# Float16 pairs for the gated layer of an attention, expert and gated-layer kernel

## The chip, the cores and the metric

The kernel runs as one program on one core of a Trainium2 chip. The metric is the device time of one execution in microseconds (us), the median of several runs. "PE" is TensorE, "PEld" its weight load, DVE is VectorE, ACT is ScalarE, POOL is GpSimd and SP is SyncE, which issues all transfers here.

## The reference

Three layers follow each other. Inputs are float32, except the three matrices of the gated layer's weights, which reach the kernel as float64 words and are turned into float32 on the chip.

```python
# attention: q, k, v (2, 8, 576, 64); heads 0-3 see 32 local positions, heads 4-7 every 32nd
attn = softmax(where(mask, q @ k.T / 8, -1e9)); x = (attn @ v) as (1152, 512)
# experts: 4 of 512 -> 1024 -> 512, all tokens through all experts
for e in range(4):
    out += p[:, e:e+1] * (maximum(x @ w1[e], 0) @ w2[e])
# gated layer: 512 -> 1536 -> 512
return (sigmoid(x @ w_gate) * (x @ w_val)) @ w_out
```

## The kernel before

**Split products.** Every float32 operand is a pair: a rounded high part and the rest as a low part. `split_products` makes one product out of three passes (high x high, high x low, low x high; L543 to L545) that add up in PSUM. The pairs are fp32r tiles (32-bit) or float16 tiles. In float16 the operand is first multiplied by a power of two that brings its largest magnitude to a fixed height, and the result is scaled back.

**Stages.** The expert layer is 8 stages `s` (4 experts, two halves of 512 hidden columns), the gated layer 3 stages `j` (512 hidden columns each). Tokens go in 3 blocks `T` of 384. A unit is a stage and a block: `g1` ("u") makes the hidden tile in 4 groups of 12 passes of 384 columns, `g2` ("d") brings it down in 4 such groups and adds it to `x2`. In the gated layer `g3` has 8 such groups (gate and value by turns), and `g4` 3 groups of 12 passes of 512 columns. The units run in the order u(s,1), d(s,0), u(s,2), d(s,1), u(s+1,0), d(s,2) and so on. Stages 0 and 1 (`EARLY` = 2) run on fp32r pairs, stages 2 to 7 on float16 pairs, the gated stages on fp32r pairs again.

**Weights.** There are 25 pieces of 512 x 512 weights. SP loads each as raw tiles of 512 KB, two to a piece in the expert stages, four (float64 words) in the gated ones; `RAW_BUFS` = 3 of these tiles exist. `prep_weights` makes the pairs: by `prep_half` for the float16 stages (two reductions for the largest magnitude, `scale_on_chip`, then per 512 columns an ACT pass and a DVE pass), by `float32_of` (five DVE passes, L323 to L332) and a copy on ACT and a subtraction on POOL (L350) for a gated tile. A prepared piece takes a buffer of each of the two tags `wh` and `wl`, of which there are five (`W_BUFS` + `W_BUFS_2`), and a float16 piece fills half of its two buffers. `prep_half` gives its two raw tiles back when the whole piece is done.

**Scale.** `scale_on_chip` has two small products: PE turns the 128 per-partition maxima into a row (L243), DVE takes the maximum and keeps its exponent, PE spreads it over the partitions (L248), DVE makes the factor and its inverse. Between the steps it says "hold", which ends the preparation for that group.

**Order.** The program is written under a manual schedule: what is emitted first comes first in each engine's queue. After the last pass of a group (`"evac"`) the loop at the end lets `prep_some` emit two steps of weight preparation (and in units 4 to 10 one step of `x_half`, the splitting of `x` for the float16 stages), and only then the group's own work on the result is emitted. A piece starts only when its buffer's last reader has been emitted (`free_after`). So PE meets a small product of a scale one group after DVE was given the reduction that it needs.

Of the kernel before, what the change touches and what calls it, by code (L numbers as in the profile page):

```python
# [22 lines left out]
TOP = 2.0 ** 14  # L23
# [15 lines left out]
def attn_moe_glu_kernel(ctx, tc, q, k, v, dp, w1, w2, wg, wv, wo, out):  # L39
# [109 lines left out]
    one = nc.const_aps.tensor(1.0, (128, 1), F32)  # L149
    SX = 2 * NST  # L150
# [76 lines left out]
    def as_half(s):  # L227

        return EARLY <= s < NST
# [3 lines left out]
    def alloc_scales():  # L233

        for name, n in (("up", SX + NT), ("down", SX + NT), ("comb", NST * NT), ("top", 2)):
# [49 lines left out]

    held_raw = {}

    def prep_half(n):
# [14 lines left out]
        pool = tmp["w"] if pool_of.get(i) == "w2" else wp  # L303
        wh[i] = pool.tile([128, 4, 512], F16, tag="wh", name="wh")
        wl[i] = pool.tile([128, 4, 512], F16, tag="wl", name="wl")
# [7 lines left out]
        for k_ in ((i, 0), (i, 2), i):  # L313
            held_raw.pop(k_)
        load_raw_to(n + 1 + RAW_BUFS)

    def float32_of(r):
# [4 lines left out]
        m = tmp["p"].tile([128, 512], U32, tag="magn", name="magn")  # L322
# [11 lines left out]
        return f.unsqueeze(1)  # L334

    def prep_weights(n):
        i, u, m = raw_list[n]
        if as_half(i // 2):
            yield from prep_half(n)
            return  # L340
        if u == 0:
            pool = tmp["w"] if pool_of.get(i) == "w2" else wp
            wh[i] = pool.tile([128, 4, 512], F32R, tag="wh", name="wh")
            wl[i] = pool.tile([128, 4, 512], F32R, tag="wl", name="wl")
        r = raw.pop((i, u))
        hi_, lo_ = wh[i][:, u:u + m, :], wl[i][:, u:u + m, :]
        if m == 1:
            r = yield from float32_of(r)
            nc.scalar.copy(hi_, r)  # L349
            nc.gpsimd.tensor_tensor(lo_, r, hi_.bitcast(F32), ALU.subtract)  # L350
        else:
            for x in range(m):
                nc.scalar.copy(hi_[:, x], r[:, x])
                yield
                nc.vector.tensor_tensor(lo_[:, x], r[:, x], hi_[:, x].bitcast(F32), ALU.subtract)
                yield
# [191 lines left out]
    def up_pairs(pc, T, fb):  # L548
        xs = (xh16, xl16) if as_half(pc // 2) else (xh, xl)
# [5 lines left out]
    def alloc_h(key):  # L555
        dt = F16 if key[0] != "g" and as_half(key[0]) else F32R
# [23 lines left out]
    def g2(s, T):  # L580
        e, pc = s // 2, 2 * s + 1
        if s == NST - 1:
            alloc_x(T)
# [6 lines left out]
        for kk in range(KC):  # L590
# [19 lines left out]
            if s == NST - 1:  # L610
                dh, dl = xh[T][:, kk, :], xl[T][:, kk, :]
                nc.scalar.copy(dh, a)
                nc.vector.tensor_tensor(dl, a, dh.bitcast(F32), ALU.subtract)
            yield "tile"

    def g3(j, T):
        base = 2 * NST + 3 * j
        alloc_h(("g", j, T))
        for fb in range(4):
# [4 lines left out]
            nc.scalar.activation(sg, pg, AF.Sigmoid)  # L624
# [6 lines left out]
            nc.vector.tensor_tensor(gv, pv_, sg, ALU.mult)  # L631
            nc.scalar.copy(dh, gv)  # L632
            nc.gpsimd.tensor_tensor(dl, gv, dh.bitcast(F32), ALU.subtract)  # L633
            yield "tile"

    def g4(j, T):
        pc, key = 2 * NST + 3 * j + 2, ("g", j, T)
# [196 lines left out]
```

## Time and profile before

| | |
|---|---|
| median of 3 runs | 716.91 us (712.18 to 731.52) |
| profiled execution, first to last instruction | 712.1 us |
| PE busy | 697.7 us |
| DVE, ACT, POOL busy | 453.4, 237.9, 211.2 us |
| granted TensorE clock, mean | 0.978 |

The profiled execution has no time of its own beside its span; the lowest run, 712.18 us, is the nearest to it. Read the table with the chain of work that ended last in mind: it runs through PE's passes up to the last addition, so time is lost where PE idles or runs at a lower clock, and where a pass takes longer than it has to.

### The profile page before, as it was taken

The page shows a single profiled execution, that of the slowest core. Times are in us where ns is not written, and L with a number is a line of the kernel's source. Part 1 is how long each engine was busy: PE and PEld are TensorE (multiplying, and loading weights), DVE is VectorE, ACT ScalarE, POOL GpSimd, SP SyncE. Part 2 cuts the span into 40 slices and gives each one's busy share as a digit, 9 for nine tenths or more (in the row PEclk, how much of TensorE's full clock was granted, in tenths as well). Part 3 has the DMA queues.
Part 4 walks back from the last instruction along what each step waited for, and adds up shares of the span by engine and source line. Part 5 has one row for each costly group of instructions (what it writes and reads, how often), then busy time and mean ns, then how long its engine had stood idle before and what let it go on. Part 6 is the DMA issues. An engine that isn't in the chain of part 4 may idle for free. (4 is left out here: it accounts for less than half of the span.)

```text
span 712.1 us, 10883 instructions
## 1 busy us (share of the span) xinstructions
PE 697.7 (98%) x4263; PEld 545.2 (77%) x4263; DVE 453.4 (64%) x857; ACT 237.9 (33%) x629; POOL 211.2 (30%) x218
## 2 busy tenths in 40 slices
PE   8999999999789999999999999999999999999998
PEld 5778889999466666656656666678999999999996
DVE  3677665888656565574565889978794777571212
ACT  4675551333313331333333222333234332221120
POOL 2452450000212222222222335542254443442120
PEclk8888999999999999999999999999999999999999
DMA  8933123021221102220121212212122123100002
GB/s 189 216 93 88 59 74 100 18 67 39 70 71 60 60 1 70 71 69 3 60 71 44 75 60 90 90 60 73 45 89 90 60 88 92 58 31 0 30 16 89
DMA packets 38940, 48.58 MB, mean 68 GB/s; under 512 B 18436, under 2 KB 23336, under 8 KB 38888
## 3 DMA queue, kind: packets, MB, share of 16 engines
q1 hardware_dynamic: 38888, 47.89, 23.3%
q8 instruction: 33, 0.54, 0.3%
q14 instruction: 19, 0.16, 0.1%
HBM read 45.50 MB, written 2.38 MB: 67 GB/s over the span
## 5 line engine op out<-in xcount | busy, mean ns | idle before, releaser
L566 POOL TENSOR_TENSOR hl<-t,hh 128x384 f16<-128x384 f32 x72 | 70.5, 984 | 248.6 <-ACT t L565 248.6
L543 PE MATMUL gps<-xh,wh 128*128 128x384 f32 x384 | 130.9, 341 | 0.4 <-DVE gv L631 0.4
L545 PE MATMUL gps<-xh,wl 128*128 128x384 f32 x384 | 128.9, 336 | 0.0
L544 PE MATMUL gps<-xl,wh 128*128 128x384 f32 x384 | 128.8, 335 | 0.0
L543 PE MATMUL gps<-hh,wh 128*128 128x384 f16 (+1 forms) x384 | 127.6, 332 | 0.6 <-ACT sg L624 0.6
L544 PE MATMUL gps<-hl,wh 128*128 128x384 f16 (+1 forms) x384 | 126.0, 328 | 0.0
L545 PE MATMUL gps<-hh,wl 128*128 128x384 f16 (+1 forms) x384 | 126.0, 328 | 0.0
L545 PE MATMUL gps<-x,wl 128*128 128x384 f16 x288 | 95.0, 330 | 0.0
L544 PE MATMUL gps<-x,wh 128*128 128x384 f16 x288 | 94.9, 329 | 0.0
L543 PE MATMUL gps<-x,wh 128*128 128x384 f16 x288 | 94.8, 329 | 0.0
L545 PEld LDWEIGHTS <-wl 128*128 128x128 f16 x576 | 56.6, 98 | 37.7 <-issue 0.7
L543 PEld LDWEIGHTS <-wh 128*128 128x128 f16 x576 | 56.5, 98 | 37.4 <-issue 1.0
L544 PEld LDWEIGHTS <-wh 128*128 128x128 f16 x576 | 56.6, 98 | 37.1 <-issue 1.3
L564 ACT ACTIVATE hh<-gps 128x384 f16<-128x384 f32 x72 | 35.3, 490 | 123.9 <-PE gps L545 123.9
L350 POOL TENSOR_TENSOR wl<-magn,wh 128x512 fp32r<-128x512 f32 x36 | 51.5, 1431 | 76.4 <-ACT wh L349 76.3
L543 PEld LDWEIGHTS gps<-xh,wh 128*128 128x128 f32 x384 | 72.4, 189 | 2.1 <-DVE gv L631 0.7
L544 PEld LDWEIGHTS gps<-xl,wh 128*128 128x128 f32 x384 | 72.4, 189 | 0.3
L545 PEld LDWEIGHTS gps<-xh,wl 128*128 128x128 f32 x384 | 72.2, 188 | 0.0
L633 POOL TENSOR_TENSOR hl<-gv,hh 128x384 fp32r<-128x384 f32 x36 | 43.0, 1194 | 96.5 <-ACT hh L632 96.4
L606 DVE SCALAR_TENSOR_TENSOR t<-gps,comb,pb 128x384 f32<-128x384 f32 x72 | 44.1, 613 | 37.6 <-PE gps L545 20.6
L631 DVE TENSOR_TENSOR gv<-gps,sg 128x384 f32<-128x384 f32 x36 | 20.0, 555 | 60.7 <-PE gps L545 55.5
L609 DVE TENSOR_TENSOR x2acc<-x2acc,t 128x384 f32<-128x384 f32 x84 | 50.9, 606 | 2.9
(113 smaller groups left out, 1073.3 us busy)
## 6 DMA issues: line engine op xcount, KB each, us to landing
raw<-in_moe_w_dram SPq DMA_DIRECT2D x32, 512.0 KB
raw<-in_moe_w_gate_dram SPq DMA_DIRECT2D x12, 512.0 KB
raw<-in_moe_w_val_dram SPq DMA_DIRECT2D x12, 512.0 KB
raw<-in_moe_w_out_dram SPq DMA_DIRECT2D x12, 512.0 KB
pb<-pd SPq DMA_DIRECT2D x11, 192.0 KB
out_dram<-outacc SPq DMA_DIRECT2D x8, 256.0 KB
vl<-in_v_dram SPq DMA_DIRECT2D x8, 160.0 KB
vs<-in_v_dram SPq DMA_DIRECT2D x4, 288.0 KB
```

The lines of the kernel that those rows point to most:

```text
L350: nc.gpsimd.tensor_tensor(lo_, r, hi_.bitcast(F32), ALU.subtract)
L543: nc.tensor.matmul(ps, ah, bh, start=i == 0, stop=False)
L544: nc.tensor.matmul(ps, ah, bl, start=False, stop=False)
L545: nc.tensor.matmul(ps, al, bh, start=False, stop=i == n - 1)
L564: nc.scalar.activation(dh, ps, AF.Relu, scale=DOWN)
L566: nc.gpsimd.tensor_tensor(dl, t, dh, ALU.subtract)
L606: nc.vector.scalar_tensor_tensor(t, ps, cc, pb[e, T], ALU.mult, ALU.mult)
L609: nc.vector.tensor_tensor(a, a, t, ALU.add)
L631: nc.vector.tensor_tensor(gv, pv_, sg, ALU.mult)
L633: nc.gpsimd.tensor_tensor(dl, gv, dh.bitcast(F32), ALU.subtract)
```

## The change

The gated layer's products go from fp32r pairs to scaled float16 pairs. For that `x2` is split by `x2_half` (two reductions, a scale, four ACT and four DVE passes per block), queued behind the last expert stage and emitted at two steps per group, with no weight preparation in those groups; before, the copy and the subtraction of `x2` stood in `g2`. A gated piece now holds four converted tiles (`magn`, five buffers), has a reduction per tile and a scale, and is split by two ACT passes and one POOL subtraction per tile. The scale is found with one bfloat16 product that carries the 128 maxima to every partition at once. A float16 piece takes one buffer for both parts, so that ten fit instead of five. A fourth raw tile exists from the end of the attention on, and `prep_half` gives its first raw tile back halfway. The factors are taken out in the sigmoid's scale, in the gated product's multiplication and in `g4`'s addition. While `x_half` runs, weights get one step per group; in the gated stages they get three.

```diff
+    late = []
+
     def load_raw_to(n):
+        n += len(late)
         while raw_next[0] < min(n, len(raw_list)):
             i, u, m = raw_list[raw_next[0]]
-            t = rawp.tile([128, m, 512], F32 if m == 2 else U64, tag="raw", name="raw")
+            pool = rawp
+            if late and (raw_next[0] - late[0]) % (RAW_BUFS + 1) == 0:
+                pool = tmp["p"]
+            t = pool.tile(
+                [128, m, 512], F32 if m == 2 else U64, tag="raw", name="raw", bufs=RAW_BUFS if pool is rawp else 1)
...
-        return EARLY <= s < NST
+        return s >= EARLY
...
     def scale_on_chip(col, m):
 
+        ps = g_tile()
+        top = m.bitcast(BF16)[:, 1:2]
+        nc.tensor.matmul(ps[:, :128], top.to_broadcast([128, 128]), identb, start=True, stop=True)
+        t = tmp["top"][:, n_top[0] % 2:n_top[0] % 2 + 1]
         n_top[0] += 1
-        t = tmp["top"][:1, n_top[0] % 2:n_top[0] % 2 + 1]
-        ps = g_tile()
-        nc.tensor.transpose(ps[:1, :128], m, ident)
-        nc.vector.tensor_reduce(t, ps[:1, :128], AX.X, ALU.max)
+        nc.vector.tensor_reduce(t, ps[:, :128], AX.X, ALU.max)
         nc.vector.tensor_scalar(t.bitcast(U32), t.bitcast(U32), 0x7F800000, None, ALU.bitwise_and)
-        yield "hold"
-        pq = g_tile()
-        nc.tensor.matmul(pq[:, :1], one[:1].to_broadcast([1, 128]), t, start=True, stop=True)
         dn = tmp["down"][:, col:col + 1]
-        nc.vector.tensor_scalar(dn, pq[:, :1], 2.0 ** -100, 1.0 / TOP, ALU.max, ALU.mult)
+        nc.vector.tensor_scalar(dn, t, 2.0 ** -100, 1.0 / TOP, ALU.max, ALU.mult)
...
+    def split_x2(steps):
+
+        while steps and gated:
+            said = next(gated[0], "end")
+            if said == "end":
+                gated.pop(0)
+            elif said == "hold":
+                return
+            steps -= 1
+
+    def x2_half(T):
+
+        pk = tmp["p"].tile([128, 3], F32, tag="xpk", name="x2pk")
+        a = acc["x2"][:, :, T * TC:(T + 1) * TC]
+        for x in range(2):
+            nc.vector.tensor_reduce(
+                pk[:, x:x + 1], a[:, 2 * x:2 * x + 2, :], AX.XY, ALU.max, apply_absolute_value=True)
+            yield
+        nc.vector.tensor_reduce(pk[:, 2:3], pk[:, :2], AX.X, ALU.max)
+        yield "hold"
+        yield from scale_on_chip(SX2 + T, pk[:, 2:3])
+        t = xp.tile([128, 2, KC, TC], F16, tag=f"xl{T}", name="x2p")
+        x2h[T], x2l[T] = t[:, 0], t[:, 1]
+        sc = tmp["up"][:, SX2 + T:SX2 + T + 1]
+        for kk in range(KC):
+            nc.scalar.activation(x2h[T][:, kk, :], a[:, kk, :], AF.Copy, scale=sc)
+            nc.vector.scalar_tensor_tensor(x2l[T][:, kk, :], a[:, kk, :], sc, x2h[T][:, kk, :], ALU.mult, ALU.subtract)
+            yield
+        x2_done.add(T)
...
+        (name, tag), = pool_of[i]
+        t = w_pool(name).tile([128, 2, 4, 512], F16, tag=tag, name="w16")
+        wh[i], wl[i] = t[:, 0], t[:, 1]
...
+            if c == 1:
+                held_raw.pop((i, 0))
+                load_raw_to(n + RAW_BUFS)
...
-        m = tmp["p"].tile([128, 512], U32, tag="magn", name="magn")
+        m = tmp["p"].tile([128, 512], U32, tag="magn", name="magn", bufs=5)
...
+    def prep_gated(n):
+
+        i, u, m = raw_list[n]
+        r = raw.pop((i, u))
+        if u == 0:
+            held_raw[i] = tmp["p"].tile([128, 5], F32, tag="gpk", name="gpk")
+        pk = held_raw[i]
+        f = held_raw[i, u] = yield from float32_of(r)
+        load_raw_to(n + 1 + RAW_BUFS)
+        nc.vector.tensor_reduce(pk[:, u:u + 1], f, AX.X, ALU.max, apply_absolute_value=True)
+        yield
+        if u < 3:
+            return
+        nc.vector.tensor_reduce(pk[:, 4:5], pk[:, :4], AX.X, ALU.max)
+        yield "hold"
+        yield from scale_on_chip(i, pk[:, 4:5])
+        (name, tag), = pool_of[i]
+        t = w_pool(name).tile([128, 2, 4, 512], F16, tag=tag, name="w16")
+        wh[i], wl[i] = t[:, 0], t[:, 1]
+        sc = tmp["up"][:, i:i + 1]
+        for c in range(4):
+            f = held_raw.pop((i, c))
+            nc.scalar.activation(wh[i][:, c, :], f, AF.Copy, scale=sc)
+            nc.scalar.activation(f, f, AF.Copy, scale=sc)
+            nc.gpsimd.tensor_tensor(wl[i][:, c, :], f, wh[i][:, c, :], ALU.subtract)
+            yield
+        held_raw.pop(i)
...
     def up_pairs(pc, T, fb):
-        xs = (xh16, xl16) if as_half(pc // 2) else (xh, xl)
+        xs = (x2h, x2l) if pc >= 2 * NST else (xh16, xl16) if as_half(pc // 2) else (xh, xl)
...
-            if s == NST - 1:
-                dh, dl = xh[T][:, kk, :], xl[T][:, kk, :]
-                nc.scalar.copy(dh, a)
-                nc.vector.tensor_tensor(dl, a, dh.bitcast(F32), ALU.subtract)
...
-            nc.scalar.activation(sg, pg, AF.Sigmoid)
+            nc.scalar.activation(sg, pg, AF.Sigmoid, scale=cg)
...
-            nc.vector.tensor_tensor(gv, pv_, sg, ALU.mult)
+            nc.vector.scalar_tensor_tensor(gv, pv_, DOWN, sg, ALU.mult, ALU.mult)
             nc.scalar.copy(dh, gv)
-            nc.gpsimd.tensor_tensor(dl, gv, dh.bitcast(F32), ALU.subtract)
+            nc.gpsimd.tensor_tensor(dl, gv, dh, ALU.subtract)
...
-                    nc.scalar.copy(a, ps)
+                    nc.scalar.activation(a, ps, AF.Copy, scale=cv)
                 else:
-                    nc.vector.tensor_tensor(a, ps, a, ALU.add)
+                    nc.vector.scalar_tensor_tensor(a, ps, cv, a, ALU.mult, ALU.add)
...
+    slots = {(name, tag): [] for name in ("w1", "w2") for tag in ("wh", "wl")}
+    bufs_of = dict(w1=W_BUFS, w2=W_BUFS_2)
+    free_after = {}
+
+    def slot_ready(slot):
+
+        occ, bufs = slots[slot], bufs_of[slot[0]]
+        if len(occ) >= bufs:
+            return last_use[occ[-bufs]]
+        return -1 if slot[0] == "w1" else N_EARLY
+
     for i in range(NP):
-        ready = {}
-        for name, bufs in (("w1", W_BUFS), ("w2", W_BUFS_2)):
-            occ = held[name]
-            ready[name] = last_use[occ[-bufs]] if len(occ) >= bufs else (-1 if name == "w1" else N_EARLY)
-        name = min(ready, key=lambda x: (ready[x], x))
-        held[name].append(i)
-        pool_of[i], free_after[i] = name, ready[name]
+        if as_half(i // 2):
+            choices = [(slot,) for slot in slots]
+        else:
+            choices = [((name, "wh"), (name, "wl")) for name in bufs_of]
+        free_after[i], pool_of[i] = min((max(map(slot_ready, c)), c) for c in choices)
+        for slot in pool_of[i]:
+            slots[slot].append(i)
...
+            if u[0] == "u" and u[1] == NST:
+                while u[2] not in x2_done:
+                    split_x2(1)
...
+                late.append(raw_next[0])
...
+                        if gated:
+                            split_x2(2)
+                            continue
                         if x16_next[0] < 2 or n > units.index(("u", EARLY - 1, x16_next[0] - 1)):
-                            next(halves, None)
-                    prep_some(n)
+                            if next(halves, "end") != "end":
+                                prep_some(n, 1)
+                                continue
+                    prep_some(n, 3 if u[1] >= NST else 2)
+            if u[0] == "d" and u[1] == NST - 1:
+                gated.append(x2_half(u[2]))
```

## Rows read from the trace of the kernel before

**Rows 1.** The page's first part: busy time, share of the span, instructions.

```profile
PE 697.7 (98%) x4263; PEld 545.2 (77%) x4263; DVE 453.4 (64%) x857; ACT 237.9 (33%) x629; POOL 211.2 (30%) x218
```

**Rows 2.** Windows: stretch, length, busy PE, PEld, DVE, ACT, POOL, clock, DMA share, GB/s.

```profile
180.00:225.00 45.00, 38.40 (x212) 25.39 (x211) 29.31 (x53) 12.98 (x26) 7.54 (x9) 0.92 0.25 79
...
470.00:515.00 45.00, 44.05 (x258) 38.34 (x256) 35.29 (x59) 16.10 (x32) 15.56 (x13) 1.00 0.19 59
515.00:642.00 127.00, 127.00 (x674) 119.75 (x673) 90.23 (x130) 39.27 (x75) 56.67 (x43) 1.00 0.23 71
```

**Rows 3.** Timeline, unit u(2,0): start, length, engine, line, operation [idle before <-releaser].

```profile
182.37 0.93 SPq L134 DMA_DIRECT2D raw<-in_moe_w_dram  x2
...
184.38 0.33 PE L545 MATMUL gps<-x,wl 128*128 128x384 f16 x1
...
187.65 1.22 DVE L295 TENSOR_REDUCE wpk<-raw 128x1 f32<-128x1024 f32 x1 [0.95 <-DMA raw<-in_moe_w_dram]
...
189.11 0.27 PE L243 MATMUL gps<-ident,wpk 128*1 128x128 f32 x1 [4.41 <-DVE wpk L300]
...
193.36 0.39 PE L544 MATMUL gps<-hl,wh 128*128 128x384 f32 x1
```

**Rows 4.** Windows of 2 us, unit u(2,0), columns as in rows 2.

```profile
190.00:192.00 2.00, 2.00 (x9) 0.84 (x6) 0.00 (x0) 0.00 (x0) 0.00 (x0) 0.52 0.00 0
```

**Rows 5.** Timeline of PE, units u(2,1) and d(2,0).

```profile
207.27 0.33 PE L545 MATMUL gps<-x,wl 128*128 128x384 f16 x1
209.79 0.27 PE L243 MATMUL gps<-ident,wpk 128*1 128x128 f32 x1 [2.19 <-DVE wpk L300]
...
214.00 0.33 PE L544 MATMUL gps<-hl,wh 128*128 128x384 f16 x1
```

**Rows 6.** Timeline of PE: float16, fp32r of 384, fp32r of 512 columns.

```profile
255.15 0.33 PE L545 MATMUL gps<-x,wl 128*128 128x384 f16 x1
...
257.10 0.33 PE L545 MATMUL gps<-x,wl 128*128 128x384 f16 x1
...
655.09 0.33 PE L545 MATMUL gps<-xh,wl 128*128 128x384 f32 x1
...
657.17 0.33 PE L545 MATMUL gps<-xh,wl 128*128 128x384 f32 x1
...
699.38 0.39 PE L545 MATMUL gps<-wh,hl 128*128 128x512 f32 x1
...
702.10 0.39 PE L545 MATMUL gps<-wh,hl 128*128 128x512 f32 x1
```

**Rows 7.** Groups of instructions, shapes apart: count, busy us, mean ns, idle before.

```profile
L609 DVE TENSOR_TENSOR x2acc<-x2acc,t 128x384 f32<-128x384 f32 x84 | 50.9, 606 | 2.9
L606 DVE SCALAR_TENSOR_TENSOR t<-gps,comb,pb 128x384 f32<-128x384 f32 x72 | 44.1, 613 | 37.6 <-PE gps L545 20.6 <-POOL hl L566 16.1
L327 DVE SCALAR_TENSOR_TENSOR bits<-raw,bits 128x512 uint32<-128x512 uint32 x36 | 32.6, 905 | 0.0
L329 DVE SCALAR_TENSOR_TENSOR bits<-raw,bits 128x512 uint32<-128x512 uint32 x36 | 31.5, 875 | 0.9
L332 DVE SCALAR_TENSOR_TENSOR magn<-magn,bits 128x512 f32<-128x512 uint32 x36 | 30.0, 835 | 0.9
L295 DVE TENSOR_REDUCE wpk<-raw 128x1 f32<-128x1024 f32 x24 | 28.4, 1211 | 12.9 <-DMA raw<-in_moe_w_dram 12.9
L325 DVE TENSOR_SCALAR magn<-raw 128x512 uint32<-128x512 uint32 x36 | 26.2, 728 | 0.0
L323 DVE TENSOR_SCALAR bits<-raw 128x512 uint32<-128x512 uint32 x36 | 20.7, 575 | 0.8
L244 DVE TENSOR_REDUCE top<-gps 1x1 f32<-1x128 f32 x15 | 4.2, 277 | 14.6 <-PE gps L243 14.6
```

**Rows 8.** Timeline of PE and of DVE in unit u(6,2).

```profile
417.98 1.40 DVE L327 SCALAR_TENSOR_TENSOR bits<-raw,bits 128x512 uint32<-128x512 uint32 x1
...
418.19 0.33 PE L545 MATMUL gps<-x,wl 128*128 128x384 f16 x1
```

More of the change, by code (lines that the diff above doesn't have):

```diff
@@ L148, in attn_moe_glu_kernel @@
     psums = const.tile([128, NTB], F32, tag="psums", name="psums")
-    one = nc.const_aps.tensor(1.0, (128, 1), F32)
-    SX = 2 * NST
+    SX = NP
+    SX2 = NP + NT
     def warm_up():
@@ L284, in x_half, with w_pool @@
                 yield
+    x2h, x2l, x2_done = {}, {}, set()
+    gated = []
+    def split_x2(steps):
[24 more added lines that the diff above has]
+        x2_done.add(T)
     held_raw = {}
+    def w_pool(name):
+        return tmp["w"] if name == "w2" else wp
     def prep_half(n):
@@ L312, in prep_half @@
             yield
-        for k_ in ((i, 0), (i, 2), i):
+            if c == 1:
+                held_raw.pop((i, 0))
+                load_raw_to(n + RAW_BUFS)
+        for k_ in ((i, 2), i):
             held_raw.pop(k_)
@@ L333, in float32_of @@
         yield
-        return f.unsqueeze(1)
+        return f
+    def prep_gated(n):
[24 more added lines that the diff above has]
+        held_raw.pop(i)
     def prep_weights(n):
         i, u, m = raw_list[n]
+        if i >= 2 * NST:
+            yield from prep_gated(n)
+            return
         if as_half(i // 2):
@@ L341, in prep_weights @@
         if u == 0:
-            pool = tmp["w"] if pool_of.get(i) == "w2" else wp
-            wh[i] = pool.tile([128, 4, 512], F32R, tag="wh", name="wh")
-            wl[i] = pool.tile([128, 4, 512], F32R, tag="wl", name="wl")
+            for d, (name, tag) in zip((wh, wl), pool_of[i]):
+                d[i] = w_pool(name).tile([128, 4, 512], F32R, tag=tag, name=tag)
         r = raw.pop((i, u))
         hi_, lo_ = wh[i][:, u:u + m, :], wl[i][:, u:u + m, :]
[L347 to L356, printed above, removed]
+        for x in range(m):
+            nc.scalar.copy(hi_[:, x], r[:, x])
+            yield
+            nc.vector.tensor_tensor(lo_[:, x], r[:, x], hi_[:, x].bitcast(F32), ALU.subtract)
+            yield
         load_raw_to(n + 1 + RAW_BUFS)
@@ L555, in alloc_h @@
     def alloc_h(key):
-        dt = F16 if key[0] != "g" and as_half(key[0]) else F32R
+        dt = F16 if key[0] == "g" or as_half(key[0]) else F32R
         Hh[key] = hp.tile([128, 4, TC], dt, tag="hh", name="hh")
@@ L581, in g2 @@
         e, pc = s // 2, 2 * s + 1
-        if s == NST - 1:
-            alloc_x(T)
         if as_half(s):
@@ L618, in g3 @@
         alloc_h(("g", j, T))
+        down = tmp["down"]
+        cg = tmp["cg"][:, j * NT + T:j * NT + T + 1]
+        nc.vector.tensor_tensor(cg, down[:, base:base + 1], down[:, SX2 + T:SX2 + T + 1], ALU.mult)
         for fb in range(4):
@@ L637, in g4 @@
         pc, key = 2 * NST + 3 * j + 2, ("g", j, T)
+        down = tmp["down"]
+        cv = tmp["cv"][:, j * NT + T:j * NT + T + 1]
+        nc.vector.tensor_scalar(
+            cv, down[:, pc - 1:pc], down[:, SX2 + T:SX2 + T + 1], 1.0 / DOWN, ALU.mult, ALU.mult)
+        nc.vector.tensor_tensor(cv, cv, down[:, pc:pc + 1], ALU.mult)
         for tb in range(NTB // NT):
@@ L685, in attn_moe_glu_kernel @@
     N_EARLY = 2 * EARLY
-    held, free_after = {"w1": [], "w2": []}, {}
-    for i in range(NP):
-        ready = {}
-        for name, bufs in (("w1", W_BUFS), ("w2", W_BUFS_2)):
-            occ = held[name]
-            ready[name] = last_use[occ[-bufs]] if len(occ) >= bufs else (-1 if name == "w1" else N_EARLY)
-        name = min(ready, key=lambda x: (ready[x], x))
-        held[name].append(i)
-        pool_of[i], free_after[i] = name, ready[name]
+    slots = {(name, tag): [] for name in ("w1", "w2") for tag in ("wh", "wl")}
[6 more added lines that the diff above has]
+        return -1 if slot[0] == "w1" else N_EARLY
+    for i in range(NP):
+        if as_half(i // 2):
[5 more added lines that the diff above has]
+            slots[slot].append(i)
     p_list, p_last = [], {}
```

7 lines of the change are left out of this document (2 added, 5 removed).

## The prediction, as it was put on record

> **What bounds the kernel now.** I read the page's busy times first: PE is busy for 697.7 of 712.1 us [rows 1], and the chain of waits runs through PE's passes to the end. So the other engines count only where PE waits for them, and the second view is the windows by stage, to see where PE idles. From 515 to 642 us (gated layer) PE is busy for all 127 us at full clock while its weight load fills 119.75 [rows 2]; so there a pass's own length decides. Two stretches idle: 180 to 225 us with 6.60 us of idle PE and a mean clock of 0.92, and 470 to 515 us with 0.95 [rows 2]. The third view, the timeline, says why the first of them idles. In u(2,0) PE stands 4.41 us at the small product of a scale. It waits for DVE's maximum, and DVE waits for a raw tile: its transfer was issued at 182.37, two tiles at once, and the second was there at 187.65 [rows 3]. SP could not issue it earlier, as three raw tiles exist and the piece before held its two until its last pass. In u(2,1) the same costs 2.19 us [rows 5]. After the first, passes that follow run at a granted clock of 0.52 [rows 4], so the price is more than the idle time.
>
> **What the two stalls cost.** From one pass to the next it takes 1.95/12 = 0.1625 us in float16, 2.08/12 = 0.1733 in fp32r of 384 columns and 2.72/12 = 0.2267 in fp32r of 512 (twelve passes each) [rows 6]. Without the first stall, 13 float16 steps and one fp32r step after 184.38 would put the second pass of d(1,2) at 186.67; it was at 193.36 [rows 3]: 6.7 us. The second: 207.27 plus 14 x 0.1625 is 209.55, and it was 214.00 [rows 5]: 4.45 us. Together 11.1 us.
>
> **Part 1, raw tiles.** With a fourth tile, and the first of a piece given back halfway, each transfer is issued before the piece in hand is done. Going through the loop at the end of the kernel group by group, the tiles of the piece that stalled first and of its neighbours (pieces 5 to 7) are now issued five or more groups ahead of the reduction that reads them. From there on, one raw tile comes about every three to four groups, seven or more groups ahead. Five groups of 1.95 us are 9.7 us; the slow pair took 187.65 - 182.37 = 5.3 us [rows 3]. While `x_half` runs, weights get one step per group instead of two, and still every piece is ready before its unit; so I take the full 11.1 us, between 4.45 (one stall stays, hidden by neither) and 11.1. What is late next there is nothing: DVE's reductions need two tiles' time, 2 x 1.21 us [rows 7], in three groups' 5.85.
>
> **Part 2, float16 passes in the gated layer.** A unit pair there has 96 passes of 384 and 36 of 512 columns, nine times. For 384 columns the gain is 0.1733 - 0.1625 = 0.0108 us, 1.04 per pair. Float16 at 512 columns is not in the trace. In fp32r 128 columns more cost 0.0534 us [rows 6]; added to the float16 pass that gives 0.2159, an estimate, and a gain of 0.0108 again, 0.39 per pair. Bounds: no gain for these 36 (nothing) and the ratio of the 384 passes, 6.2% or 0.0141 us (0.51). Taken: 9 x (1.04 + 0.39) = 12.8 us, between 9.4 and 14.0. All of it is on the path, for PE never idles there. The Trainium skill ("TensorE: Matmul & The Clock Gate", section "Back-to-back issue gap") gives the gap as columns over 2.4 GHz plus 2.5 ns whatever the type; the float16 row agrees (162.5 ns), the fp32r row (173.3) does not. By that rule both types would cost the same, and part 2 would be zero; it is a rival below.
>
> **Part 3, the scale.** Before there were 15 scales of two products, now 27 of one: 30 small products against 27, taken as nothing. What counts is when PE meets them. The twelve new ones (nine gated pieces, three blocks of `x2`) stand in PE's queue one group after DVE was given the last reduction. If DVE is behind by more than a group, PE waits, and all later passes wait behind it. So DVE's load decides.
>
> **Part 4, DVE's load.** A gated piece costs four conversions of 0.575 + 0.728 + 0.905 + 0.875 + 0.835 = 3.92 us, or 15.7 [rows 7]. New are four reductions of 512 columns, half of L295's 1.21 each, 2.4 us, and five small operations of at most L244's 0.277, 1.4 us. The POOL subtraction stays; a second ACT pass per tile fits, as ACT is busy for 39 of 127 us [rows 2]. In the expert stages, at two steps per group, a piece takes 16 groups, 31.2 us of PE. In these DVE also has eight additions of 0.613 + 0.606 us, 9.8 [rows 7]. Sum 29.3 of 31.2, or 94%. In the gated stages, at three steps, a piece takes one unit pair: 96 x 0.1625 + 36 x 0.2159 = 23.4 us. DVE has 15.7 + 2.4 + 1.4 and four gated products of some 0.61, sum 21.9, also 94%. So DVE keeps up over a piece, but inside a "d" unit it falls behind and catches up in the "u" unit after it. The nearest row for the lateness: in u(6,2) DVE in the kernel before, at the same load per group, did a conversion from 417.98 to 419.38 that was emitted with the first group, while PE ended the third group's passes at about 418.35 [rows 8]. A scale product at the new place would have waited some 1.1 us. That conversion took 1.40 instead of 0.905, beside POOL's subtractions, which the change issues after the scale, not before it. I take 0.25 us for each of the twelve, 3.0 us, between 0 and 1.2 each (14.4). Weight buffers are no limit: with ten slots every piece is split well before its unit.
>
> **Part 5, `x2`.** A copy on ACT and a subtraction on DVE per group leave `g2`; per block two reductions, a scale and four splits come, queued behind it. For the first block they end in d(7,1), one unit ahead of u(8,0); the others have more. The 0.95 us of idle PE in that stretch [rows 2] lies around the first sigmoid; I take half back, 0.5, between 0 and 0.95. In the groups that emit these steps no weights are prepared (some 16 groups); the pieces for u(8,x) are done by then, so the cover is there; without it PE would wait for a piece.
>
> **The sum.** 712.1 - 11.1 - 12.8 - 0.5 + 3.0 = 690.7 us for the profiled execution. That execution is as long as the lowest of the three runs; the median is 4.7 us above it, for no reason that the trace shows. By the median the same 21.4 us give 695.5. I take the middle, 693.
>
> **Rivals.** *DVE becomes the bound* (0.14): each of the twelve scale products waits 1.2 us, 14.4 instead of 3.0, and the span is 702.1, with the median's half offset 704.4. For it speaks the 94%, and the late conversion [rows 8]; against it that each wait of PE lets DVE catch up. The Trainium skill ("SBUF — State Buffer", section "Who interferes with whom") says that a DVE instruction with two SBUF inputs and a GpSimd instruction that reads SBUF exclude each other for the whole instruction; the conversion of 1.40 us [rows 8] agrees. *The float16 passes are no shorter* (0.03): in these stages the pass is as long as its columns, which both types share, and part 2 is nothing: 690.7 + 12.8 = 703.5, or 705.8. Against it stands the difference of the float16 and fp32r rows [rows 6]. It is what the gap rule of the Trainium skill in part 2 would give. *The raw tile is still late once* (0.05): one stall of 6.7 us stays, 697.4, or 699.7. *Slower* (0.04): DVE's lateness at the scales reaches the 2.19 us at which the trace shows PE to lose 4.45 [rows 5], because the clock falls after it; at all twelve that is 53 us, 687.7 + 53 = 741. It decides from about 1 us more lateness per scale than the late conversion shows [rows 8]; a conversion would have to cost 4.3 us, not 3.92, so that DVE's sum passes PE's 31.2.
>
> **How the numbers follow.** The forecast has 0.74. Its own range goes from 687 (no new wait, profile basis) to 699 (6 us of waits, median basis); taking the size of the 512-column gain in, 685. To hold 8 in 10 it must reach to the first two rivals, 706. Two per cent, about what a measurement can tell from no change here, is 702.6. Faster by more: the forecast, the late raw tile and some of the DVE rival, 0.84. Within: the rest of that and the float16 rival, 0.12. Slower: 0.04.
>
> **What would show it.** Right: no wait of PE for a reduction around 180 to 215 us and a clock of 1.00 there; groups of 1.95 us in `g3` and of 2.59 in `g4`; waits of PE at the line of the new product that add up to some 3 us, DVE at over 90% from 320 to 590 us. Wrong: these waits at 1 us or more each with the clock falling behind them, a raw transfer issued less than 5 us ahead of its reduction, or gated groups still at 2.08 us.

## The result and the profile after

The changed kernel has a median of 695.76 us (686.17 to 705.02, 4 runs), the kernel before 714.54 us in the same measurement; the ratio is 0.9633, 95% interval 0.9548 to 0.9718: faster. The forecast was 693 us, 685 to 706. The profiled execution took 687.93 us, with a span of 686.1. The median is the middle of two runs at 686.17 and 687.93 us and two at 703.59 and 705.02, whose mean granted clock was lower (0.954 and 0.951 against 0.983 and 0.980) and which the ratio leaves out.

To compare kernels below 1% I count from one place, the first float16 pass of u(2,0), up to the end of the span: what lies ahead of it took between 169.0 and 198.7 us in the executions of this study, and what lies behind it repeats to 0.1 us (508.5 in both traces of the changed kernel). It is called "from the mark". The timeline of PE in the changed kernel, with the mark, the first gated pass and the last pass:

```profile
177.62 0.34 PE L614 MATMUL gps<-x,w 128*128 128x384 f16 x1
...
462.85 0.33 PE L614 MATMUL gps<-x2p,w 128*128 128x384 f16 x1
...
682.15 0.27 PE L616 MATMUL gps<-w,hl 128*128 128x256 f16 x1
```

In the kernel before, the same three passes start at 178.68, 474.76 and 708.48 us of 712.1.

| us | before | after | change |
|---|---|---|---|
| ahead of the mark | 178.7 | 177.6 | -1.1 |
| mark to first gated pass | 296.1 | 285.2 | -10.9 |
| first gated pass to last pass | 233.7 | 219.3 | -14.4 |
| last pass to end | 3.6 | 4.0 | +0.3 |
| from the mark | 533.4 | 508.5 | -24.9 |

The page's first part answers to [rows 1], and its chain still runs through PE:

```profile
PE 675.5 (98%) x4244; PEld 447.0 (65%) x4245; DVE 489.9 (71%) x986; ACT 269.9 (39%) x665; POOL 196.4 (29%) x218
...
PE 90%; DVE 6%; DMA 1%; issue 1%; POOL 1%; SPq 0%; ACT 0%; POOLq 0%; DVEq 0%; ACTq 0%
```

DVE has 36.5 us more to do, and the time is shorter all the same. The windows (columns as in [rows 2]) show where PE stands:

```profile
180.00:225.00 45.00, 43.26 (x266) 29.14 (x265) 33.70 (x62) 17.89 (x36) 10.97 (x12) 1.00 0.32 91
320.00:460.00 140.00, 139.53 (x860) 83.41 (x859) 123.47 (x220) 55.32 (x108) 55.89 (x52) 1.00 0.22 66
460.00:590.00 130.00, 130.00 (x759) 73.77 (x758) 112.85 (x201) 54.84 (x93) 42.10 (x37) 1.00 0.20 61
```

Between 180 and 225 us PE now idles for 1.74 us, not 6.60 [rows 2], at a clock of 1.00. From 320 to 590 us DVE is busy for 236.3 of 270 us (88%), and PE idles for 0.47. All waits of PE behind 150 us (engine, line, releaser: sum, times, longest):

```profile
PE gps L250 <- DVE wpk L343: 1.7, 1, 1.7
PE gps L250 <- DVE gpk L395: 0.7, 1, 0.7
PE gps L250 <- DVE x2pk L314: 0.5, 1, 0.5
```

All three are at the new small product of a scale, and none is for a weight. The timeline of PE at these three places:

```profile
183.43 0.23 PE L250 MATMUL gps<-identb,wpk 128*128 128x128 bf16 x1 [1.74 <-DVE wpk L343]
183.50 0.33 PE L614 MATMUL gps<-x,w 128*128 128x384 f16 x1
...
453.03 0.23 PE L250 MATMUL gps<-identb,x2pk 128*128 128x128 bf16 x1 [0.47 <-DVE x2pk L314]
453.10 0.33 PE L614 MATMUL gps<-x,w 128*128 128x384 f16 x1
...
596.51 0.23 PE L250 MATMUL gps<-identb,gpk 128*128 128x128 bf16 x1 [0.68 <-DVE gpk L395]
596.58 0.38 PE L614 MATMUL gps<-w,hh 128*128 128x512 f16 x1
...
599.17 0.38 PE L614 MATMUL gps<-w,hh 128*128 128x512 f16 x1
```

Two of them are the x2 scale and a gated scale; the 1.74 us at u(2,0) is what is left of the stall of [rows 3]. The next pass starts 0.07 us after the small product. From 596.58 to 599.17 lie twelve float16 passes of 512 columns: 2.59 us, 0.2158 each. The timeline of DVE ahead of the first of the three waits:

```profile
179.37 1.21 DVE L338 TENSOR_REDUCE wpk<-raw 128x1 f32<-128x1024 f32 x1
180.50 0.55 DVE L677 TENSOR_TENSOR t<-gps,pb 128x384 f32<-128x384 f32 x1
181.07 0.98 DVE L678 TENSOR_TENSOR x2acc<-x2acc,t 128x384 f32<-128x384 f32 x1
181.98 1.21 DVE L338 TENSOR_REDUCE wpk<-raw 128x1 f32<-128x1024 f32 x1
183.22 0.16 DVE L343 TENSOR_REDUCE wpk<-wpk 128x1 f32<-128x2 f32 x1
```

No reduction waits for a transfer any more, as L295 did in [rows 3]: the second one is late because DVE did a group's additions before it. One sign that the prediction named, no wait of PE for a reduction around 180 to 215 us, thus did not hold.

### The profile page after: what moved, and what is told of

It is laid out like the page before. It is cut to its first block, busy times and chain, and to the rows that moved or that the text cites. A ratio compares the mean times of both kernels' runs of the same rounds, so it can differ in the third digit from the quotient of the medians.

```text
span 686.1 us, 10981 instructions
## 1 busy us (share of the span) xinstructions
PE 675.5 (98%) x4244; PEld 447.0 (65%) x4245; DVE 489.9 (71%) x986; ACT 269.9 (39%) x665; POOL 196.4 (29%) x218
## 4 chain that ended last, share of the span: by engine, by line
PE 90%; DVE 6%; DMA 1%; issue 1%; POOL 1%; SPq 0%; ACT 0%; POOLq 0%; DVEq 0%; ACTq 0%
PE gps L614 27%; PE gps L616 27%; PE gps L615 27%; PE sps L485 2%; PE tps L528 2%; PE sps L498 2%; PE o L549 1%; DMA ks<-in_k_dram 1%; PE qkps L466 1%; DVE x2acc L678 1%; PE qkps L444 1%; DVE wpk L338 1%; DVE x L289 1%; DVE magn L371 1%; DVE t L288 0%
## 5 line engine op out<-in xcount | busy, mean ns | idle before, releaser
L614 PEld LDWEIGHTS <-w 128*128 128x128 f16 x864 | 84.5, 98 | 56.1 <-issue 0.3
L616 PEld LDWEIGHTS <-w 128*128 128x128 f16 x864 | 84.5, 98 | 55.9
L615 PEld LDWEIGHTS <-w 128*128 128x128 f16 x864 | 84.5, 98 | 55.0
L614 PE MATMUL gps<-x,w 128*128 128x384 f16 x288 | 93.9, 326 | 0.0
L615 PE MATMUL gps<-x,w 128*128 128x384 f16 x288 | 93.9, 326 | 0.0
L616 PE MATMUL gps<-x,w 128*128 128x384 f16 x288 | 93.9, 326 | 0.0
L614 PE MATMUL gps<-hh,w 128*128 128x384 f16 x288 | 93.9, 326 | 0.0
L615 PE MATMUL gps<-hl,w 128*128 128x384 f16 x288 | 93.9, 326 | 0.0
L616 PE MATMUL gps<-hh,w 128*128 128x384 f16 x288 | 93.9, 326 | 0.0
L614 PE MATMUL gps<-x2p,w 128*128 128x384 f16 x288 | 93.9, 326 | 0.0
L615 PE MATMUL gps<-x2p,w 128*128 128x384 f16 x288 | 93.9, 326 | 0.0
L616 PE MATMUL gps<-x2p,w 128*128 128x384 f16 x288 | 93.9, 326 | 0.0
L701 POOL TENSOR_TENSOR hl<-gv,hh 128x384 f16<-128x384 f32 x36 | 34.7, 965 | 146.0 <-ACT hh L700 146.0
L354 DVE SCALAR_TENSOR_TENSOR w<-raw,up,w 128x512 f16<-128x512 f32 x48 | 38.3, 798 | 20.3 <-ACT w L352 20.3
L512 ACT ACTIVATE P<-sps,nm 72x72 f32<-72x72 f32 (+1 forms) x112 | 36.4, 331 | 36.3 <-DVE nm L510 20.6
L699 DVE SCALAR_TENSOR_TENSOR gv<-gps,sg 128x384 f32<-128x384 f32 x36 | 19.9, 554 | 40.6 <-PE gps L616 40.3
L406 POOL TENSOR_TENSOR w<-magn,w 128x512 f16<-128x512 f32 x36 | 45.7, 1274 | 9.3 <-ACT magn L405 8.9
```

Source lines behind the costliest of these rows:

```text
L354: nc.vector.scalar_tensor_tensor(wl[i][:, c, :], part, sc, wh[i][:, c, :], ALU.mult, ALU.subtract)
L406: nc.gpsimd.tensor_tensor(wl[i][:, c, :], f, wh[i][:, c, :], ALU.subtract)
L512: nc.scalar.activation(pp[:, j, :], pv_[:, j, :], AF.Exp, bias=nm[:n, j:j + 1], accum_out=sm[:n, j:j + 1])
L614: nc.tensor.matmul(ps, ah, bh, start=i == 0, stop=False)
L615: nc.tensor.matmul(ps, ah, bl, start=False, stop=False)
L616: nc.tensor.matmul(ps, al, bh, start=False, stop=i == n - 1)
```

## The experiments

Twelve runs follow. The first four take the change apart; "before" and "after" in a heading say which kernel was edited.

**e1: before, with the raw tiles alone.** The fourth tile and the early return, nothing else.

```diff
+        n += len(late)
...
+            if late and (raw_next[0] - late[0]) % (RAW_BUFS + 1) == 0:
+                pool = tmp["p"]
...
+            if c == 1:
+                held_raw.pop((i, 0))
+                load_raw_to(n + RAW_BUFS)
```

> The kernel before with the raw tiles' part of the change alone: a fourth tile from the end of the attention on, and the first tile of a piece given back halfway. Theory (the two stalls of u(2,0) and u(2,1) are late raw tiles, and their price is idle PE plus the low clock after it): both go, the span falls from 712.1 by 9 to 11 us to 701 to 703, with a clock of 1.00 from 180 to 225 us. Rival (the stalls went because the weights got one step per group beside the splitting of x, or because a scale has one product): they stay, and the span is 710 to 713.

Measured: 708.22 us (702.37 to 728.28, ratio 0.9883, 0.9782 to 0.9983); from the mark 526.9, that is -6.5 against before, not -11.1. The second stall is gone, the first is not. The waits of PE, then the timeline of DVE at the first stall:

```profile
PE gps L250 <- DVE wpk L307: 3.4, 1, 3.4
```
```profile
178.59 0.61 DVE L289 SCALAR_TENSOR_TENSOR t<-xh,up,x 128x384 f32<-128x384 f32 x1
179.24 1.36 DVE L290 SCALAR_TENSOR_TENSOR x<-xl,up,t 128x384 f16<-128x384 f32 x1
180.53 2.33 DVE L302 TENSOR_REDUCE wpk<-raw 128x1 f32<-128x1024 f32 x2
182.90 0.15 DVE L307 TENSOR_REDUCE wpk<-wpk 128x1 f32<-128x2 f32 x1
```

Both reductions run back to back from 180.53 without waiting for data; ahead of them DVE splits `x` (L289, L290). In the kernel before, DVE itself stood idle for the transfer for 0.95 us at the first stall [rows 3], and for 4.18 us at the second. The timeline of DVE there:

```profile
208.23 1.22 DVE L295 TENSOR_REDUCE wpk<-raw 128x1 f32<-128x1024 f32 x1 [4.18 <-DMA raw<-in_moe_w_dram]
```

So the second stall was the transfer's, and went with it. The first was the transfer's by about 0.95 of its 4.41 us; the rest was DVE, which came late to the reductions, and 3.36 us stayed.

**e2: after, without the raw tiles.** The same lines taken out.

> The changed kernel without the raw tiles' part: three tiles, both of a piece given back at its end. Theory: the stalls come back, and as ten slots let the preparation run on without pause, at more pieces than two; eleven expert pieces whose second tile comes 4 to 6 us before its scale's product, 1 to 4.5 us each: span 697 to 735 us. Rival (pace and the single product took the stalls away): 686 to 690 us.

Measured: 689.06 us (686.15 to 709.57, ratio 0.9628, 0.9552 to 0.9705); from the mark 511.5, +3.1 against after. The timeline of PE shows the wait at u(2,0) as it is in the changed kernel, and two others in its place further on; the timeline of SP and of DVE is of the larger one:

```profile
183.77 0.23 PE L250 MATMUL gps<-identb,wpk 128*128 128x128 bf16 x1 [1.74 <-DVE wpk L343]
...
267.22 0.23 PE L250 MATMUL gps<-identb,wpk 128*128 128x128 bf16 x1 [0.50 <-DVE wpk L343]
...
276.39 0.95 SPq L141 DMA_DIRECT2D raw<-in_moe_w_dram  x2
...
281.74 1.22 DVE L338 TENSOR_REDUCE wpk<-raw 128x1 f32<-128x1024 f32 x1 [4.12 <-DMA raw<-in_moe_w_dram]
...
283.21 0.23 PE L250 MATMUL gps<-identb,wpk 128*128 128x128 bf16 x1 [2.11 <-DVE wpk L343]
```

So of the 11.1 us that I gave to the raw tiles, 3.1 come back without them, and not at the old place: there something else in the change has removed the stall. The mechanism at the new place is that of the second stall of before: a pair of tiles comes 5.3 us after its issue, and DVE idles for 4.12 us.

**e3: before, with float16 gated tiles and no scale.** It leaves the scale of the gated layer out, so its low parts lose digits; the number and shape of passes are those of the changed kernel.

```diff
-            wh[i] = pool.tile([128, 4, 512], F32R, tag="wh", name="wh")
-            wl[i] = pool.tile([128, 4, 512], F32R, tag="wl", name="wl")
+            dt = F32R if i < 2 * NST else F16
+            wh[i] = pool.tile([128, 4, 512], dt, tag="wh", name="wh")
+            wl[i] = pool.tile([128, 4, 512], dt, tag="wl", name="wl")
```

> The kernel before with float16 tiles in the gated layer in place of fp32r, without any scale (the low parts lose digits; order, loads and the rest as before). Theory (a float16 pass starts 0.0108 us sooner than an fp32r one at 384 and at 512 columns, and the switches between the two types cost 0.1 to 0.2 us each): 24.87 us per unit pair fall to 23.4, nine times, and some 0.7 us for the switches: 712.1 - 14 = 698 us. Rival (the pass is as long as its columns, the gain in the gated layer came from fewer waits): 711 to 712 us, pairs at 24.9.

Measured: 702.01 us (700.07 to 718.82, ratio 0.9819, 0.9727 to 0.9912); from the mark 520.3, -13.1. Both stalls of before are still there (4.25 and 2.56 us). So the type alone is worth some 13 us, beside the stalls. From the first gated pass to the end it is 223.1 us against 237.3 before, 14.2 less, as in the changed kernel (223.3); 1.1 is lost ahead of it. The 0.7 us that I expected for the switches between the types isn't in the traces: in before, the last float16 pass, at 474.74 us, is followed by the first fp32r pass after 0.02 and by the second after 0.31 more, together no longer than one undisturbed gap of each type.

**e4: after, one more group ahead of every scale's product.** If lateness of DVE is what PE waits for at L250, a group more should hide it.

```diff
         yield "hold"
+        yield "hold"
         yield from scale_on_chip(i, pk[:, 4:5])
```

(the same in `prep_half` and `x2_half`)

> The changed kernel with one more group between the last reduction of a weight piece or of a block of x2 and the small product of its scale. Theory (the three waits of PE at that product, 1.74, 0.47 and 0.68 us, are DVE's lateness of less than one group): they go, 686.1 - 2.9 = 683.2 us. Rival (DVE is full over the piece, so the wait moves to the next scale): 685 to 687 us with waits of the same sum at other pieces.

Measured: 695.22 us (688.92 to 712.64, ratio 0.9699, 0.9607 to 0.9790); from the mark 518.1, +9.7 against after. From the mark to the first gated pass it takes 282.2 us, 3.0 less than after: there the waits are gone. In the gated stages it takes 12.8 more:

```profile
PE gps L619 <- POOL w L409: 6.6, 6, 1.8
PE gps L250 <- DVE gpk L397: 1.7, 1, 1.7
PE gps L617 <- ACT w L407: 0.7, 1, 0.7
```

These waits are 9.0 us, and the clock falls beside them (0.89 from 520 to 535 us, 0.83 from 600 to 610). A second "hold" gives a group of preparation away at each scale, and at the end the weights themselves are late (L407, L409 write them). So there is little slack in the preparation.

**e5: after, with the scale's two old products.**

```diff
-        nc.tensor.matmul(ps[:, :128], top.to_broadcast([128, 128]), identb, start=True, stop=True)
+        nc.tensor.transpose(ps[:1, :128], m, ident)
...
+        yield "hold"
+        pq = g_tile()
+        nc.tensor.matmul(pq[:, :1], one[:1].to_broadcast([1, 128]), t, start=True, stop=True)
```

> The changed kernel with the scale of before: two small products, one group apart. Compared from the first float16 pass of u(2,0) to the end of the span (508.5 us in the changed kernel, since what lies ahead of it differs by up to 10 us between executions). Theory after the runs so far (a pair of old products costs PE 0.3 us against 0.07 for the new one, and one group more per piece makes the preparation late, as in the run with a later scale): 6 us for 24 scales and 8 to 12 us of waits for unready weights, 521 to 527 us. Rival (the prediction's: 30 small products against 27 are nothing): 508 to 510 us.

Measured: 727.43 us (727.33 to 727.66; before 731.46, no interval); the mark comes only at 195.39 us, so what lies behind it is compared: 530.4, +21.9 against after, more than either theory gave. The waits of PE, and the timeline of PE at one scale without a wait:

```profile
PE gps L619 <- POOL w L409: 5.4, 6, 1.2
PE gps L257 <- DVE top L254: 1.5, 2, 0.8
PE gps L252 <- DVE gpk L398: 1.4, 2, 1.1
PE gps L252 <- DVE wpk L346: 1.4, 1, 1.4
```
```profile
350.35 0.33 PE L619 MATMUL gps<-x,w 128*128 128x384 f16 x1
350.51 0.27 PE L252 MATMUL gps<-ident,wpk 128*1 128x128 f32 x1
350.62 0.33 PE L617 MATMUL gps<-hh,w 128*128 128x384 f16 x1
...
352.41 0.33 PE L619 MATMUL gps<-hh,w 128*128 128x384 f16 x1
352.67 0.38 PE L257 MATMUL gps<-top,const-float32-1.0 1*128 1x1 f32 x2
352.98 0.34 PE L617 MATMUL gps<-hh,w 128*128 128x384 f16 x1
```

From 350.35 to 350.62 it is 0.27 us with the first product between, instead of 0.1625, and from 352.41 to 352.98 it is 0.57 with the second: the pair costs PE some 0.51 us, the new product 0.057. For the 22 scales behind the mark that is about 10 us. The waits are 10.2 us against 2.9 of after (0.5 at `x2pk` in both), 7.3 more, 5.4 of them for weights, which fits a group given away at each second product. Of the remaining 4.7 us, some 3.4 by estimate are stretches of lower clock (0.97 from 560 to 620 us, 0.98 from 620 to 700); the rest is not assigned.

**e6: after, with each gated tile reduced twice.** Twice the same maximum: 36 x 0.681 us = 24.5 us more for DVE to do, with order and the rest unchanged.

```diff
-        nc.vector.tensor_reduce(pk[:, u:u + 1], f, AX.X, ALU.max, apply_absolute_value=True)
+        for _ in range(2):
+            nc.vector.tensor_reduce(pk[:, u:u + 1], f, AX.X, ALU.max, apply_absolute_value=True)
```

> The changed kernel with each gated tile reduced twice, the second time for nothing: 36 x 0.68 = 24.5 us more on DVE, order and the rest unchanged. From the first float16 pass of u(2,0) on, 508.5 us in the changed kernel. Theory of the prediction (DVE is at 94% of PE's time over a piece): 2.7 us more per piece puts it over, 32.0 against 31.2 and 24.6 against 23.4, and PE waits at the scales: 511 to 518 us. Rival (there is room, as the windows show DVE at 88 to 92%): under 510.5 us.

Measured: 717.58 us (702.66 to 718.13, no interval); from the mark 523.1, +14.6. The waits of PE, the busy times of its page, then two of its windows:

```profile
PE gps L250 <- DVE gpk L396: 10.2, 6, 2.6
```
```profile
PE 679.9 (97%) x4245; PEld 447.7 (64%) x4245; DVE 502.8 (72%) x1022; ACT 270.2 (39%) x665; POOL 197.1 (28%) x218
```
```profile
360.00:380.00 20.00, 17.82 (x104) 10.30 (x103) 17.96 (x36) 5.47 (x12) 6.56 (x6) 0.94 0.29 87
...
440.00:460.00 20.00, 17.84 (x101) 10.19 (x100) 14.77 (x28) 9.32 (x18) 8.79 (x8) 0.91 0.14 38
```

All waits behind the mark are 13.2 us against 2.9, and the clock falls behind some of them. More came of it than I expected. And the edit did less than it says: DVE is busy for 12.9 us more than in the changed kernel (502.8 against 489.9), not 24.5, since other passes of its got shorter, L371 above all (517 ns each, 738 in the changed kernel). The 14.6 us behind the mark are thus more than DVE really got: 10.3 are waits, and some 3.0, by estimate from the clock in the two windows, its fall.

**e7, e11: after, one more group at three scales only,** those at which PE waited: piece 6 (stage 3), block 0 of `x2`, piece 24.

```diff
         yield "hold"
+        if i == 6:
+            yield "hold"
         yield from scale_on_chip(i, pk[:, 2:3])
```

(and `T == 0` in `x2_half`, `i == 24` in `prep_gated`)

> The changed kernel with one more group ahead of the scale's product at three places alone, those where PE waited: weight piece 6, block 0 of x2, weight piece 24. Theory (these waits, 2.9 us, are a lateness of less than a group, and the run with a later scale everywhere lost by the preparation's pace, 21 groups in all): from the first float16 pass of u(2,0) on 505.6 us against 508.5, without a wait for weights. Rival (any group given away is paid back by late weights or by the next scale): 508 us or more.

Measured: 690.79 us (678.76 to 699.67, no interval); from the mark 504.6, -3.9 against after. No wait is left behind the mark. It beats both kernels from the mark, so it was run again beside the changed kernel, each with its own profile:

> The run with a later scale at three places again, beside the changed kernel on the same chip, for the time. Theory: from the first float16 pass on 504.6 us again, and 3 to 4 us less than the changed kernel between runs of the same first 180 us. Rival: no difference beyond 1 us.

> The changed kernel again on the same chip as the run before. Theory: 508.5 us from the first float16 pass on, whatever the first 180 us do; the whole span moves with the clock granted in the first 100 us alone. Rival: what lies behind the first float16 pass differs between executions by more than 1 us too.

e11: 691.97 us (682.77 to 699.98), ratio 0.9569, 0.9505 to 0.9633; e12: 686.84 us (683.73 to 705.15), ratio 0.9603, 0.9555 to 0.9651. The ratios overlap; they are 0.0034 apart, some 2.4 us, the way that was expected. The medians stand the other way round, since four of six runs of e12 and three of six of e11 were below 690 us. From the mark it is 504.6 again, against 508.5 again. That the three waits cost 3.9 us is shown by the traces; the run times don't separate the two.

**e8: after, without the raw tiles and without the new pace.** While `x_half` runs, weights get two steps again.

```diff
-                            if next(halves, "end") != "end":
-                                prep_some(n, 1)
-                                continue
+                            next(halves, None)
```

> The changed kernel without the raw tiles' part, and with the old pace while x is split (two steps of weights beside one of x, not one). Theory (the slower pace took the weight pieces out of the crowd on DVE ahead of u(2,0), and took the stalls away where the raw tiles' part was missing): the stalls of before come back, 4 and 2 us of idle PE with a clock of 0.5 after them; from the first float16 pass on 511.5 + 6 to 11, that is 517 to 523 us. Rival (ten slots and the single product did it): 511 to 513 us.

Measured: 695.35 us (694.94 to 712.58, no interval); from the mark 512.1, but a wait of 2.63 us lies just ahead of it here, so with it 514.8. That is 6.3 more than after, between the two theories, and 3.2 more than e2, which lacks the raw tiles but has the new pace. Behind that wait there are four for gated maxima (2.7 us in all) and two for those of `x2` (1.7), where the changed kernel has one of each (0.7 and 0.5), and the clock from 198 to 210 us is 0.86.

**e9: before, with the new pace alone.** The lines of e8 the other way round.

> The kernel before with the new pace alone: one step of weights per group while x is split, not two. From the first float16 pass of u(2,0) to the end, 533.4 us before. By the order of emission the second raw tile of pieces 6, 7 and 8 is still issued one group ahead of its reduction, and the small product comes two groups after the issue. Theory (late raw tiles are a cause of their own): three or four waits of 2 to 4 us at the small product with a low clock after them, 533 to 541 us. Rival (the crowd on DVE ahead of u(2,0) is the whole cause): 522 to 526 us.

Measured: 702.71 us (one run); from the mark 525.6, -7.8 against before. My theory, that the pace alone brings nothing, fell, and 525.6 is in the range of the rival, the crowd on DVE. With three raw tiles as before, one stall of 1.41 us is left, where there were 4.41 and 2.19, and the clock stays at 1.00 behind it (184 to 192 us). At the second place the transfer is late as before, and DVE idles for 3.40 us, but here PE reaches the product later and doesn't wait:

```profile
184.65 0.27 PE L243 MATMUL gps<-ident,wpk 128*1 128x128 f32 x1 [1.41 <-DVE wpk L300]
...
200.16 1.22 DVE L295 TENSOR_REDUCE wpk<-raw 128x1 f32<-128x1024 f32 x1 [3.40 <-DMA raw<-in_moe_w_dram]
...
201.63 0.27 PE L243 MATMUL gps<-ident,wpk 128*1 128x128 f32 x1
```

**e10: before, with the single product alone.** The lines of e5 the other way round.

> The kernel before with the new scale alone (one bfloat16 product, one group less per piece). From the first float16 pass on, 533.4 us before. By the order of emission the product of piece 8 then comes four groups after its raw tile is issued, that of piece 7 two groups. Theory: the second stall goes (4.4 us), the first stays, and eighteen small products in the expert stages cost 1.9 us less: 526 to 529 us. Rival (both stalls are DVE's, or both are the raw tile's with the same lead): both stay or both go, 531 to 532 or 520 to 522 us.

Measured: 720.07 us (one run; 194.96 us lie ahead of the mark); from the mark 523.3, -10.1, between theory and rival. The first stall stays, at 2.43 us, and the second goes, as the theory had it. The reductions ahead of the wait start 2.8 us behind the mark (at 197.74), where they started 6.8 us behind it in before, and none of them waits for a transfer.

```profile
201.46 0.23 PE L242 MATMUL gps<-identb,wpk 128*128 128x128 bf16 x1 [2.43 <-DVE wpk L298]
```

## Why the prediction was right, and which of its steps were not

The sum was 21.4 us; from the mark it was 24.9, so the terms are right in sum and not one by one. The gaps from one PE pass to the next, in the timelines of both kernels from the mark to the last pass, added up by kind and set against undisturbed ones, give the terms:

| us | predicted | measured |
|---|---|---|
| the two stalls, their idle time and low clock | -11.1 | 11.15 less two pairs of small products: -10.15 |
| small products of the scale | 0 | 9 x 0.505 = -4.5, 22 x 0.057 = +1.25 |
| waits at the new product | +3.0 | +3.35 |
| float16 passes in the gated layer | -12.8 | -14.0 |
| gated layer's waits for ACT and DVE | -0.5 | -1.6 |
| last pass to end | 0 | +0.3 |
| sum | -21.4 | -25.3 (-24.9 by the marks) |

**The raw tiles (part 1): right in the time, wrong in the cause.** The stalls are gone but for 1.74 us, as predicted to within 2 us. But "I take the full 11.1 us" for the raw tiles fell, and that the time came out is luck: the change carries two more repairs of the same stalls. Each of three parts alone takes more than half of it: from the mark, e1 (raw tiles) brings 6.5, e9 (pace) 7.8, e10 (single product) 10.1, of which about 4.0 is the small products' own time (9 x 0.45). The 24.4 us that these three add up to are more than the two stalls and the small products hold, 10.15 + 4.0. And without the raw tiles only 3.1 come back (e2), at other pieces. The first stall is set by the later of two things, the transfer and DVE's queue; I read the releaser of the reduction in [rows 3], a DMA, and stopped there. The same row has the size that I overlooked: DVE idled for the transfer for 0.95 us, while PE stood for 4.41. Behind it stood DVE, crowded by `x_half`, and that is where 3.36 us stayed in e1. Only the second stall, with 4.18 us of idle DVE, was the transfer's. "What is late next there is nothing" was the sentence that failed; the pace, which I had down as something the raw tiles could bear, is a part of the gain. How the single product removes stalls was seen (4.41 and 2.19 in before, 2.43 in e10); that the reductions start some 4 us earlier there is seen too, and that this comes of the group saved per piece is argued.

**The float16 passes (part 2): right, and somewhat small.** The 858 undisturbed fp32r gaps of 384 columns have a mean of 0.1742 us and the 312 of 512 columns 0.2278, above the twelve that I took from [rows 6] (0.1733, 0.2267); in float16 it is 0.1625 and 0.2159. 858 x 0.0117 + 312 x 0.0119 + 0.24 for the passes of 256 columns are 14.0 us. The estimate for 512 columns in float16, 0.2159, was exact. The rival of passes that are no shorter is out: e3, where the type is all that changes, gains 13.1. The Trainium skill ("TensorE: Matmul & The Clock Gate", section "Back-to-back issue gap") gives some 216 ns for 512 columns by its rule, which it calls the gap of an isolated product and sets against 131 measured in a stream; the float16 rows, a stream, agree with the 216 and not with the 131, and the fp32r rows lie 12 ns above the rule.

**The scale (part 3): "30 small products against 27, taken as nothing" was mis-sized.** It counted products, not their time on PE. An old pair lengthens the gaps between passes by 0.107 + 0.40 us, a new product by 0.057. That is 3.3 us net behind the mark. In e5, with the old pair, the weights are late as well, for 5.4 us.

**DVE (part 4): right in the sum of waits, partly by luck.** I had 94% load for DVE and 0.25 us for each of twelve new waits. Two of the twelve waited, 0.47 and 0.68 us, and the passes behind them came 1.4 us late in all; the other 1.9 us of the +3.35 are the rest of the old stall, so the new waits are half of the 3.0. DVE is at 88%, not "over 90%". The conversion of a tile takes 3.81 us for 3.92 estimated, the new reduction 0.681 for 0.61. (By the prediction's own sum a conversion would have to cost 4.4 us, not 4.3, to pass PE's 31.2.) The reading of [rows 8] had a slip: the POOL work beside the late conversion was L566, two subtractions of the hidden tile from 416.53 to 418.82 us, which the change leaves in place, and not the weights' subtraction L350. The rival "DVE becomes the bound" did not come true, but e6 shows how near it is: 12.9 us more of busy DVE, and 10.3 us more of waits with lower clock behind some of them. "Weight buffers are no limit: with ten slots every piece is split well before its unit" holds in the changed kernel, yet with less in hand than "well before" says: e4 and e5 wait 5 to 7 us for weights as soon as each scale gives one group away.

**`x2` (part 5): right in sign.** Before, the gated layer's two waits lengthened the gaps around them by 1.6 us, not by the 0.95 of idle time alone; both are gone. That the work on `x2` caused them is not shown: e3 leaves that work in place, and one wait of 0.64 us is left there.

**The median.** I added half of the unexplained 4.7 us between the profiled execution and the median. Other runs of the kernel before at 716.5 to 717.6 us have a mean clock of 0.974, those at 711 to 713 of 0.978 to 0.981; so it is likely the clock at the start, which the last section shows in traces of the changed kernel. That 695.76 came so near to 693 is luck: it is the middle of two far pairs of runs, while the profiled span, 686.1, lies 4.6 below the 690.7 of the sum.

## What to carry to other kernels

A stall can have two causes in line, and the releaser of the instruction names only the later one: compare the idle time beside it with the whole stall (0.95 of 4.41 us here), and follow the queue of that engine before giving the stall to one repair. Price a small product by the gap between the passes around it: a float32 transpose with a one-row broadcast took 0.51 us of PE, a bfloat16 product that does both 0.057. Where an engine runs at 88% beside the bound, put off only the steps at which the bound was seen to wait (e7, -3.9 us); put off everywhere, the same step cost 9.7 us (e4).

## What was not expected of the hardware

The time ahead of the mark goes with the granted clock in the first 100 us. The same window in two executions of the changed kernel, e12 and then the one profiled at first:

```profile
0.00:100.00 100.00, 96.78 (x649) 75.54 (x650) 48.76 (x152) 48.68 (x227) 32.19 (x57) 0.66 0.49 113
```
```profile
0.00:100.00 100.00, 96.16 (x782) 76.16 (x783) 61.31 (x188) 57.87 (x269) 41.85 (x69) 0.86 0.50 120
```

PE was busy for 96 to 97 us in both, and in e12 it did 649 instructions in place of 782. The mark comes at 194.81 us in e12 and at 177.62 in the other. In e4 the window has 0.97 and the mark is at 168.96. So one and the same kernel differs by 17 us between executions, and the runs at 686 and at 704 us differ by as much. What sets the clock at the start isn't shown by any run.

An idle stretch of PE was not followed by a lower clock each time. After 4.41 us in before it was 0.52 [rows 4], and around the 2.43 us of e10 the clock from 200 to 210 us was 0.83; around 3.36 us in e1 and 1.74 in the changed kernel it stayed at 1.00 (183 to 200 us in both). In e6 it is 0.72 from 376 to 382 us, around an idle stretch of 2.18, and 1.00 from 611 to 617, around one of 2.57. What decides stays open.
